# Squared-ReLU attention and a gated MLP on one core: the two key blocks of a pair share their keys in turn, queue order and buffers change

## The chip, the cores and the metric

One core of a Trainium2 chip runs the kernel. The metric is the device time of one launch in microseconds (us), from runs of the whole program. Five instruction streams run side by side: TensorE (PE, with its weight loads as PEld), VectorE (DVE), ScalarE (ACT), GpSimd (POOL) and SyncE (SP), which here issues nearly every DMA. Each works through its own instructions in order and waits for the others by semaphores.

## The reference

```python
scores = (1.0 / S) * np.matmul(z, z.transpose(0, 2, 1))   # z: 4 x 3008 x 64
attn = np.maximum(scores, 0.0) ** 2
x = (u * np.matmul(attn, v)).reshape(B * S, D)             # u, v: 4 x 3008 x 256
gate = 1.0 / (1.0 + np.exp(-(x @ w_gate)))                 # x: 12032 x 256, w_gate, w_val: 256 x 1536
out = (gate * (x @ w_val)) @ w_out                         # w_out: 1536 x 256
```

`u`, `v`, `z` are float32; the three weights are float64, and the kernel reads them as pairs of 32-bit words. The matrix of scores is symmetric, since both factors are z.

## The kernel before

Attention. Each of 4 batches has 6 chunks of queries (512, the last 448) and 12 pairs of key blocks (256 keys, the last pair 192). A step (b, c, i) is one pair i against one chunk c; there are 288, listed in `steps`, 12 for each chunk. TensorE makes the scores in two terms (lines 338, 339), ScalarE takes ReLU and square into a ring buffer `r` of four slots (346, 347), ScalarE or VectorE rounds to a high part `ah` (360, 362), VectorE forms the low part `al` (367), and TensorE multiplies both with the high and low parts of v (452, 454, 459). A chunk's sums stay in two banks of PSUM until `keep` copies them to DRAM (471, 472).

Symmetry is used. Where a pair's block e = i // 2 lies past the chunk c, the step's `r` is also wanted, transposed, by a later chunk. `turn` lets VectorE transpose 32 x 32 squares into one of six buffers `turned` (414), and `store` writes them by four DMAs to the DRAM tile `shared` (389). In the later chunk the step is mirrored: no scores are made, and `load_back` reads the block into its slot of `r` by two DMAs (429). `half` does the same for one quarter of the diagonal block (405, 423). In chunk (0, 0), called late, `r` is stored untransposed and turned after its read-back (434). In a row of the shared tile the 128 keys of one block lie side by side, so a store writes runs of 32 floats and a read-back reads runs of 128.

One turn g of the main loop emits: scores of step g + 2, the transpose and the stores of step g + 1, jobs listed in `before`, square and rounding of step g + 2, `keep` for a chunk that has ended, the read-back of step g + 4, jobs listed in `after`, and the products of step g. SP meets its DMAs in that order. Among the jobs are the loads of z and v for the next batch (into few raw buffers, 288) and 18 objects `Narrow`: each loads 512 KB of float64 weight words (178) in turn g, in turn g + 1 ScalarE takes their absolute value (183), and some turns later the float32 high and low parts are stored to DRAM (229, 230). They start at steps 24 to 52, 84 to 126 and 156 to 191, so batch 3 has none.

The gated MLP (called GLU in the code) follows in 12 groups of up to 1024 rows, six turns J each; its 12 pieces of weights `w_gv` and 6 of `w_o` are reloaded around the end of the attention (560, 562, 569). Rows of u and the sums are loaded a group ahead (497, 508). VectorE joins the products (610, 612) in ring order of four PSUM banks, and at a group's end `finish` transposes the outputs into `osb` (655), from where 16 DMAs write them (658); the second half (t = 1) uses the same two places as the first.

Of the kernel before, what the change touches and what calls it, by code (L numbers as in the profile page):

```python
# [26 lines left out]
def kernel(  # L27
# [10 lines left out]
    nc = tc.nc  # L38
# [15 lines left out]
    def chunk(c):  # L54
# [7 lines left out]
        "v": 68, "z": 28, "zq": 4, "r": 16, "ah": 12, "al": 8, "al2": 4,  # L62
# [49 lines left out]
    def shared(b, c, e):  # L112

        return e > c and ((b, c) != (0, 0) or e > 2)
# [5 lines left out]
    def order(b, c):  # L120
# [8 lines left out]
        own.sort(key=lambda i: (i // 2 != c, i))  # L129
# [29 lines left out]
    class Narrow:  # L159
# [64 lines left out]
        def parts(self):  # L224
# [4 lines left out]
            nc.sync.dma_start(dst[:, 0], f32(self.hi[:, 0:n]))  # L229
            nc.sync.dma_start(dst[:, 1], f32(self.lo[:, 0:n]))  # L230

        jobs = ("load", "abs", "shift", "sign", "low_words", "add", "sums", "parts")
# [45 lines left out]
    def v_place(b, i):  # L278
        n = (b * NPAIR + i) % 17
        hi, lo = part(v_a, 2 * n, CH, F32R), part(v_a, 34 + 2 * n, CH, F32R)  # L280
        return (ap.rearrange("p (j d) -> p j d", j=2) for ap in (hi, lo))

    def load_v(b, i):
# [3 lines left out]
        if i < NPAIR - 1:  # L287
            nc.sync.dma_start(t, v[b, k0 : k0 + 256, :].rearrange("(j p) d -> p j d", p=P))
# [25 lines left out]
    def r_of(s):  # L314
        return ring(r_a, 4, 4, s)

    def a_of(s):
        n = number[s] % 3
        al = part(al_a, 4 * n, 4 * KB, F32R) if n < 2 else part(al2_a, 0, 4 * KB, F32R)
        return ring(ah_a, 4, 3, s, F32R), al.rearrange("p (j q) -> p j q", j=2)  # L320

# [3 lines left out]
    def pe_scores(s):  # L325
# [10 lines left out]
        for j in range(2):  # L336
            o = (i % 2) * 256 + j * P
            nc.tensor.matmul(sc[:, j, 0 : n - q0], kh[:, o : o + P], q, start=True, stop=False)  # L338
            nc.tensor.matmul(sc[:, j, 0 : n - q0], kl[:, o : o + P], q, start=False, stop=True)  # L339
# [42 lines left out]
    shared_t, half_t = {}, {}  # L382

    def store(dst, t):

        rows = dst.rearrange("j (T p) q -> p (j T) q", p=32)
        for g in range(4):
            src = t[32 * g : 32 * g + 32].rearrange("p (T q) -> p T q", q=32)
            nc.sync.dma_start(rows[:, :, 32 * g : 32 * g + 32], src)  # L389
# [6 lines left out]
    def turn(s):  # L396
# [3 lines left out]
        e, r = i // 2, r_of(s)  # L400
        if halved(b, c) and i == 2 * c:
            half_t[b, c] = dram.tile([2, CH // 2, P], F32, name=f"half_{b}_{c}")
            t = turned(CH)
            for j in range(2):
                nc.vector.transpose(out=t[:, j * 256 : j * 256 + 256], in_=r[:, j, CH // 2 : CH])
            store(half_t[b, c], t)
        if shared(b, c, e):
            if (b, c, e) not in shared_t:
                shared_t[b, c, e] = dram.tile([4, CH, P], F32, name=f"shared_{b}_{c}_{e}")
# [529 lines left out]
```

## Time and profile before

| | us |
|---|---|
| median of 3 runs (lowest, highest) | 2238.66 (2236.91, 2243.06) |
| the profiled execution's own time | 2240.36 |
| its span, first to last instruction | 2238.6 |
| busy: TensorE, VectorE, ScalarE, GpSimd | 2018.6, 1362.7, 1106.3, 367.1 |

The span is read from one profiled execution; its time is 1.7 us above the median of the runs. TensorE's busy time is no measure of useful work alone, since a matmul takes twice as long at the lower of its two clock levels. TensorE's mean granted clock over the span is 0.956 of full speed. The attention fills about the first half of the span and the GLU the second.

### The profile page before, as it was taken

To read this page: it belongs to the slowest core of one execution; us is meant where nothing else is said; L and a number is where in the kernel's file an instruction comes from. 1 tells how busy PE (TensorE), PEld (TensorE's weight loads), DVE (VectorE), ACT (ScalarE), POOL (GpSimd) and SP (SyncE) were. 2 spreads that over 40 slices of the span, in tenths; PEclk is the share of its full clock that TensorE was granted. 3 is DMA by queue.
4 is the path that set the end of the run, shared out by engine and by line. 5 is a ranking of instruction groups with operands and counts; after the bars stand their busy time and mean duration, and the time that the engine had idled before them with its cause. 6 is when DMAs were issued, how large, how long until landed. Compare 5 with 4: busy or idle time off the path is not lost.

```text
span 2238.6 us, 25947 instructions
## 1 busy us (share of the span) xinstructions
PE 2018.6 (90%) x9078; PEld 1736.4 (78%) x9078; DVE 1362.7 (61%) x1719; ACT 1106.3 (49%) x1428; POOL 367.1 (16%) x293
## 2 busy tenths in 40 slices
PE   9987797886997779999699999999999999999998
PEld 7765586765876668887588888887888888888888
DVE  7565575665665556654466666566575666756654
ACT  8754375654666556775344334343343434434333
POOL 0000000000000000000023233232333332333323
PEclk9998999888998999999899999999999999999999
DMA  8786788877898877997841121111212112120110
GB/s 146 132 179 158 185 172 169 183 178 183 184 162 184 193 188 173 169 178 179 254 150 36 23 49 35 29 31 26 47 33 34 29 29 48 29 38 22 27 19 15
DMA packets 948611, 240.57 MB, mean 107 GB/s; under 512 B 780160, under 2 KB 922496, under 8 KB 948480
## 3 DMA queue, kind: packets, MB, share of 16 engines
q1 hardware_dynamic: 944224, 238.39, 49.4%
q8 instruction: 71, 1.16, 0.2%
q10 hardware_dynamic: 4256, 0.52, 0.1%
q14 instruction: 60, 0.49, 0.1%
HBM read 130.55 MB, written 102.24 MB: 104 GB/s over the span
## 4 chain that ended last, share of the span: by engine, by line
PE 61%; DMA 12%; SPq 10%; ACT 8%; DVE 5%; issue 4%; ACTq 0%; DVEq 0%
PE banks L587 10%; PE banks L589 10%; PE banks L588 10%; PE banks L648 5%; PE banks L649 5%; PE banks L647 5%; PE banks L452 4%; PE banks L459 4%; PE banks L454 4%; DMA r<-shared 4%; SPq L389 3%; ACT ah L362 3%; ACT r L347 2%; ACT r L346 2%; SPq L429 2%
## 5 line engine op out<-in xcount | busy, mean ns | idle before, releaser
L631 POOL TENSOR_TENSOR h<-spare,h 128x512 fp32r<-128x512 f32 (+1 forms) x288 | 366.7, 1273 | 1861.9 <-ACT h L626 1861.9
L452 PE MATMUL banks<-ah,v 128*128 128x512 f32 (+1 forms) x1152 | 457.9, 401 | 136.9 <-ACT ah L362 126.4
L367 DVE TENSOR_TENSOR al<-r,ah 128x1024 fp32r<-128x1024 f32 (+1 forms) x287 | 344.1, 1200 | 350.3 <-ACT ah L362 341.6
L454 PE MATMUL banks<-ah,v 128*128 128x512 f32 (+1 forms) x1104 | 434.5, 394 | 0.0
L459 PE MATMUL banks<-al,v 128*128 128x512 f32 (+1 forms) x1152 | 361.4, 397 | 25.5 <-DVE al L367 21.0
L452 PEld LDWEIGHTS banks<-ah,v 128*128 128x128 f32 x1152 | 230.8, 200 | 188.4 <-ACT ah L362 146.8
L622 DVE TENSOR_TENSOR spare<-banks,spare 128x512 f32<-128x512 f32 (+1 forms) x288 | 195.6, 679 | 287.5 <-PE banks L589 287.1
L362 ACT ACTIVATE ah<-r 128x1024 fp32r<-128x1024 f32 (+1 forms) x251 | 258.0, 1034 | 180.1 <-DMA r<-shared 139.0
L618 ACT ACTIVATE spare<-spare 128x512 f32<-128x512 f32 (+1 forms) x288 | 179.1, 622 | 326.5 <-DVE spare L612 320.3
L626 ACT ACTIVATE h<-spare 128x512 fp32r<-128x512 f32 (+1 forms) x288 | 178.6, 620 | 229.6 <-DVE spare L622 226.4
L459 PEld LDWEIGHTS banks<-al,v 128*128 128x128 f32 x1152 | 224.5, 199 | 77.0 <-DVE al L367 48.6
L454 PEld LDWEIGHTS banks<-ah,v 128*128 128x128 f32 x1104 | 222.4, 201 | 27.4
L346 ACT ACTIVATE r<-banks 128x1024 f32<-128x1024 f32 (+1 forms) x171 | 164.1, 959 | 41.5 <-PE banks L339 40.8
L347 ACT ACTIVATE r<-r 128x1024 f32<-128x1024 f32 (+1 forms) x171 | 172.0, 1006 | 5.4
L587 PE MATMUL banks<-z,v 128*128 128x512 f32 x414 | 157.2, 380 | 0.0
L589 PE MATMUL banks<-z,v 128*128 128x512 f32 x414 | 157.0, 379 | 0.0
L588 PE MATMUL banks<-z,v 128*128 128x512 f32 x378 | 143.3, 379 | 0.0
L338 PE MATMUL banks<-zq,z 128*128 128x512 f32 (+2 forms) x344 | 126.6, 371 | 10.4 <-DMA zq<-z 9.9
L612 DVE TENSOR_TENSOR spare<-banks,zt 128x512 f32<-128x512 f32 (+1 forms) x144 | 114.4, 794 | 31.8 <-PE banks L589 31.7
L612 DVE TENSOR_TENSOR spare<-banks,spare 128x512 f32<-128x512 f32 (+1 forms) x144 | 115.7, 804 | 27.3 <-PE banks L589 24.4
L587 PE MATMUL banks<-v 128*128 128x512 f32 (+1 forms) x342 | 126.9, 371 | 0.0
L588 PE MATMUL banks<-v 128*128 128x512 f32 (+1 forms) x342 | 126.7, 370 | 0.0
(120 smaller groups left out, 3235.6 us busy)
## 6 DMA issues: line engine op xcount, KB each, us to landing
r<-shared SPq DMA_DIRECT2D x220, 256.0 KB, 3.9
shared<-turned SPq DMA_DIRECT2D x292, 128.0 KB, 3.3
shared<-spare SPq DMA_DIRECT2D x148, 128.0 KB, 3.4
turned<-sums SPq DMA_DIRECT2D x22, 512.0 KB, 4.0
turned<-in_u_dram SPq DMA_DIRECT2D x176, 64.0 KB, 2.3
out_dram<-osb SPq DMA_DIRECT2D x176, 64.0 KB, 1.9
sums<-keep SPq DMA_DIRECT2D x20, 512.0 KB, 3.6
raw<-in_v_dram SPq DMA_DIRECT2D x33, 256.0 KB, 4.2
```

The source lines that it names most:

```text
L346: nc.scalar.activation(by_halves(r[:, :, q0:n]), products(sc[:, :, 0 : n - q0]), AF.Relu, scale=scale)
L347: nc.scalar.activation(r[:, :, q0:n], r[:, :, q0:n], AF.Square)
L362: nc.scalar.activation(ah[:, :, 0:n], r[:, :, 0:n], AF.Copy)
L367: nc.vector.tensor_tensor(al[:, :, 0:n], r[:, :, 0:n], f32(ah[:, :, 0:n]), op=ALU.subtract)
L452: nc.tensor.matmul(o, vh[:, j, ds], moving(ah[:, j, 0:n]), start=(k == 0 and j == 0), stop=False)
L454: nc.tensor.matmul(o, vl[:, j, ds], moving(ah[:, j, 0:n]), start=False, stop=False)
L459: nc.tensor.matmul(acc[:, d, 0:n], vh[:, j, ds], moving(al[:, j, 0:n]), start=False, stop=stop)
L587: nc.tensor.matmul(o, wt[:, 0, w], xh, start=(x == 0), stop=False)
L588: nc.tensor.matmul(o, wt[:, 0, w], xl, start=False, stop=False)
L589: nc.tensor.matmul(o, wt[:, 1, w], xh, start=False, stop=end)
L612: nc.vector.tensor_tensor(by_half(g_t[dst][:, 0:m]), product(bank(J, value, name)), product(other), op=ALU.add)
L631: nc.gpsimd.tensor_tensor(lo[:, 0:m], g_t[c][:, 0:m], f32(hi[:, 0:m]), op=ALU.subtract)
```

## The change

The keys of a pair are dealt to its two blocks in turn: key 2p goes to the first block and 2p + 1 to the second (the last pair stays as it was). The scores' weights are read with a step of two, v is loaded as two neighbouring rows to a partition, and the transposes write their squares interleaved. A shared tile is now 512 x 512 with whole rows, so a store writes runs of 64 floats (of 32 in the last pair), and one DMA reads a block back with two neighbouring rows to a partition. `r` has five slots for four, the v ring 16 places for 17, and block 5 of chunk (0, 0) is computed again and not shared. The late stores are issued by GpSimd.

In a turn, the read-back comes first and is that of step g + 5; then the store of a chunk's sums, one turn after its copy; then the stores of step g, transposed the turn before. The parts of narrowed weights are stored a turn later, at its end. Some of the last weights have other places and load at other times, and `finish` puts its second half into `t_p`. The diff, without its unchanged lines:

```diff
@@ -59,7 +59,7 @@
-        "v": 68, "z": 28, "zq": 4, "r": 16, "ah": 12, "al": 8, "al2": 4,
+        "v": 64, "z": 28, "zq": 4, "r": 20, "ah": 12, "al": 8, "al2": 4,
@@ -111,7 +111,7 @@
-        return e > c and ((b, c) != (0, 0) or e > 2)
+        return e > c and ((b, c) != (0, 0) or e in (3, 4))
@@ -126,7 +126,7 @@
-        own.sort(key=lambda i: (i // 2 != c, i))
+        own.sort(key=lambda i: (i // 2 > c, i // 2 < c and c < NCH - 1, i))
@@ -226,10 +226,15 @@
-            nc.sync.dma_start(dst[:, 0], f32(self.hi[:, 0:n]))
-            nc.sync.dma_start(dst[:, 1], f32(self.lo[:, 0:n]))
-        jobs = ("load", "abs", "shift", "sign", "low_words", "add", "sums", "parts")
+            self.done = [(dst[:, 0], f32(self.hi[:, 0:n])), (dst[:, 1], f32(self.lo[:, 0:n]))]
+        def store(self):
+            for dst, src in self.done:
+                nc.sync.dma_start(dst, src)
+        jobs = ("load", "abs", "shift", "sign", "low_words", "add", "sums", "parts", "store")
@@ -276,8 +281,8 @@
-        n = (b * NPAIR + i) % 17
-        hi, lo = part(v_a, 2 * n, CH, F32R), part(v_a, 34 + 2 * n, CH, F32R)
+        n = (b * NPAIR + i) % 16
+        hi, lo = part(v_a, 2 * n, CH, F32R), part(v_a, 32 + 2 * n, CH, F32R)
@@ -285,7 +290,7 @@
-            nc.sync.dma_start(t, v[b, k0 : k0 + 256, :].rearrange("(j p) d -> p j d", p=P))
+            nc.sync.dma_start(t, v[b, k0 : k0 + 256, :].rearrange("(p j) d -> p j d", j=2))
@@ -312,12 +317,17 @@
-        return ring(r_a, 4, 4, s)
+        return ring(r_a, 4, 5, s)
+    def keys_of(i, ap, j):
+        if i == NPAIR - 1:
+            return ap[:, j * P : j * P + P]
+        return ap.rearrange("p (n j) -> p j n", j=2)[:, j]
@@ -334,9 +344,10 @@
-            o = (i % 2) * 256 + j * P
-            nc.tensor.matmul(sc[:, j, 0 : n - q0], kh[:, o : o + P], q, start=True, stop=False)
-            nc.tensor.matmul(sc[:, j, 0 : n - q0], kl[:, o : o + P], q, start=False, stop=True)
+            o = (i % 2) * 256
+            h, l = (keys_of(i, ap[:, o : o + 256], j) for ap in (kh, kl))
+            nc.tensor.matmul(sc[:, j, 0 : n - q0], h, q, start=True, stop=False)
+            nc.tensor.matmul(sc[:, j, 0 : n - q0], l, q, start=False, stop=True)
@@ -379,14 +390,23 @@
-    shared_t, half_t = {}, {}
-    def store(dst, t):
-        rows = dst.rearrange("j (T p) q -> p (j T) q", p=32)
+    shared_t, half_t, turned_t = {}, {}, {}
+    def rows_of(d):
+        return d.rearrange("(T p) q -> p T q", p=32)
+    def store(dst, i, q0, t):
+        rows = rows_of(dst)
-            src = t[32 * g : 32 * g + 32].rearrange("p (T q) -> p T q", q=32)
-            nc.sync.dma_start(rows[:, :, 32 * g : 32 * g + 32], src)
+            src = t[32 * g : 32 * g + 32].rearrange("p (T q) -> p T q", q=64)
+            if i < NPAIR - 1:
+                nc.sync.dma_start(rows[:, :, q0 + 64 * g : q0 + 64 * g + 64], src)
+            else:
+                for j in range(2):
+                    q = q0 + P * j + 32 * g
+                    if q < chunk(NCH - 1):
+                        nc.sync.dma_start(rows[:, :, q : q + 32], src[:, :, 32 * j : 32 * j + 32])
@@ -397,41 +417,62 @@
-        e, r = i // 2, r_of(s)
+        e, r = i // 2, r_of(s).rearrange("p j (T a) -> p T j a", a=32)
-            half_t[b, c] = dram.tile([2, CH // 2, P], F32, name=f"half_{b}_{c}")
-            t = turned(CH)
-            for j in range(2):
-                nc.vector.transpose(out=t[:, j * 256 : j * 256 + 256], in_=r[:, j, CH // 2 : CH])
-            store(half_t[b, c], t)
-        if shared(b, c, e):
+            turned_t[s, "half"] = t = turned(CH)
+            nc.vector.transpose(out=t.rearrange("p (T b j) -> p T j b", j=2, b=32), in_=r[:, 8:16])
+        if shared(b, c, e) and not late(b, c):
+            turned_t[s] = t = turned(2 * CH)
+            lie = "p (T b j) -> p T j b" if i < NPAIR - 1 else "p (T j b) -> p T j b"
+            nc.vector.transpose(out=t.rearrange(lie, j=2, b=32), in_=r)
+    def store_turned(s):
+        b, c, i = s
+        if back(s):
+            return
+        e = i // 2
+        if (s, "half") in turned_t:
+            half_t[b, c] = dram.tile([CH // 2, CH // 2], F32, name=f"half_{b}_{c}")
+            store(half_t[b, c], 0, 0, turned_t.pop((s, "half")))
+        if not shared(b, c, e):
+            return
+        if late(b, c):
-                shared_t[b, c, e] = dram.tile([4, CH, P], F32, name=f"shared_{b}_{c}_{e}")
-            dst = shared_t[b, c, e][2 * (i % 2) : 2 * (i % 2) + 2]
-            t = r.rearrange("p j q -> p (j q)")
-            if not late(b, c):
-                src, t = t, turned(2 * CH)
-                nc.vector.transpose(out=t, in_=src)
-            store(dst, t)
+                shared_t[b, c, e] = dram.tile([CH // 2, 2 * CH], F32, name=f"shared_{b}_{c}_{e}")
+            rows, r = rows_of(shared_t[b, c, e]), r_of(s)
+            for g in range(4):
+                for j in range(2):
+                    o = 64 * (8 * (i % 2) + 2 * g + j)
+                    src = r[32 * g : 32 * g + 32, j].rearrange("p (T a) -> p T a", a=64)
+                    nc.gpsimd.dma_start(rows[:, :, o : o + 64], src)
+        else:
+            if (b, c, e) not in shared_t:
+                shared_t[b, c, e] = dram.tile([CH, CH], F32, name=f"shared_{b}_{c}_{e}")
+            store(shared_t[b, c, e], i, (i % 2) * 256, turned_t.pop(s))
+    def as_stored(i):
+        return part(keep_a, 4 * (i % 2), 2 * CH)
+        r = r_of(s)
-            r = r_of(s)
-            for j in range(2):
-                dst = r[:, j, 0 : CH // 2].rearrange("p (i q) -> p i q", q=P)
-                nc.sync.dma_start(dst, half_t[b, c][:, j * P : j * P + P, :].rearrange("i p q -> p i q"))
+            nc.sync.dma_start(r[:, :, 0 : CH // 2], half_t[b, c].rearrange("(p j) q -> p j q", j=2))
-            r = part(keep_a, 4 * (i % 2), 2 * CH).rearrange("p (j q) -> p j q", j=2) if late(b, i // 2) else r_of(s)
-            for j in range(2):
-                k0 = (i % 2) * 256 + j * P
-                dst = r[:, j].rearrange("p (i q) -> p i q", q=P)
-                nc.sync.dma_start(dst, shared_t[b, i // 2, c][:, k0 : k0 + P, :].rearrange("i p q -> p i q"))
+            n, d = chunk(c), shared_t[b, i // 2, c]
+            if late(b, i // 2):
+                nc.sync.dma_start(as_stored(i), d[P * (i % 2) : P * (i % 2) + P])
+            else:
+                rows = d[256 * (i % 2) : 256 * (i % 2) + 256].rearrange("(p j) q -> p j q", j=2)
+                nc.sync.dma_start(r[:, :, 0:n], rows[:, :, 0:n])
-            nc.vector.transpose(out=r_of(s).rearrange("p j q -> p (j q)"), in_=part(keep_a, 4 * (i % 2), 2 * CH))
+            src = as_stored(i).rearrange("p (B j a k) -> p k B j a", j=2, a=32, k=2)
+            dst = r_of(s).rearrange("p k (B b j) -> p k B j b", b=32, j=2)
+            for k in range(2):
+                nc.vector.transpose(out=dst[:, k], in_=src[:, k])
@@ -463,13 +504,15 @@
-    def keep(b, c):
+    def keep(b, c, store):
-        nc.scalar.activation(by_halves(t[:, :, 0:n]), products(acc_of(b, c)[:, :, 0:n]), AF.Copy)
-        nc.sync.dma_start(sums[:, :, t0 : t0 + n], t[:, :, 0:n])
+        if store:
+            nc.sync.dma_start(sums[:, :, t0 : t0 + n], t[:, :, 0:n])
+        else:
+            nc.scalar.activation(by_halves(t[:, :, 0:n]), products(acc_of(b, c)[:, :, 0:n]), AF.Copy)
@@ -547,9 +590,9 @@
-            a, o = v_a, (0, 28, 32, 36, 40, 44)[F]
+            a, o = v_a, (0, 4, 32, 36, 8, 12)[F]
-            a, o = (second("w", "wgv"), 7 * F) if F < 3 else (v_a, 4 + 7 * (F - 3))
+            a, o = (second("w", "wgv"), 7 * F) if F < 3 else (v_a, (16, 23, 40)[F - 3])
@@ -562,7 +605,7 @@
-        a, o = (v_a, 64) if F == 0 else (ah_a, 4 * (F - 1)) if F < 4 else (al_a, 4 * (F - 4))
+        a, o = (second("r", "x"), 16) if F == 0 else (ah_a, 4 * (F - 1)) if F < 4 else (al_a, 4 * (F - 4))
@@ -651,7 +694,7 @@
-        osb = part(second("al2", "osb"), 2 * h, CH)
+        osb = t_p[:, 2 + h] if t else part(second("al2", "osb"), 2 * h, CH)
@@ -678,13 +721,17 @@
+                if (b, p) == (1, 1):
+                    g = 5 * NPAIR + 3
+            for i in range(1, NPAIR):
+                line[i] = max(line[i], line[i - 1] + 1)
-                g = g0 + (2 * NPAIR + 4, 2 * NPAIR + 8, 3 * NPAIR + 2, 3 * NPAIR + 7, 4 * NPAIR + 6)[i] if i < 5 else line[i - 5]
+                g = g0 + (2 * NPAIR + 4, 2 * NPAIR + 8, 3 * NPAIR + 2, 3 * NPAIR + 7)[i] if i < 4 else line[i - 4]
@@ -696,7 +743,7 @@
-                at(after if x == 0 else before, g + x, getattr(job, name))
+                at(after if name in ("load", "store") else before, g + x, getattr(job, name))
@@ -708,7 +755,6 @@
-        at(after, g + 2, load_o, 0)
@@ -789,6 +835,11 @@
+            if g + 5 < len(steps):
+                load_back(steps[g + 5])
+            if k == 1 and g > 1:
+                keep(*steps[g - 2][:2], True)
+            store_turned(steps[g])
```

SP in batch 1, chunk 1, steps 90 to 93, before. `shared_1_5` is the tile of chunk 1 and block 5, `turned` and `spare` hold transposed squares, `w` the words of a narrowing job, and the row on `in_moe_w_gate_dram` is the load of one:

```order
L429 DMA r<-shared_0_1_1895 128x4x128 x2
L389 DMA shared_1_3_2258<-turned 32x32x32 x8
L389 DMA shared_1_4_2328<-spare 32x32x32 x8
L429 DMA r<-shared_0_1_1895 128x4x128 x2
L271 DMA zq<-z 64x512
L272 DMA zq<-z 64x512
L389 DMA shared_1_5_2384<-turned 32x32x32 x4
L229 DMA w_o<-w 128x512
L230 DMA w_o<-w 128x512
L423 DMA r<-half_1_2174 128x2x128 x2
L178 DMA w<-in_moe_w_gate_dram 128x2x512
L389 DMA shared_1_5_2384<-turned 32x32x32 x4
```

The same place after:

```order
L467 DMA r<-shared_0_1_1910 128x1024
L460 DMA r<-half_1_2189 128x2x256
L404 DMA shared_1_4_2343<-spare 32x16x64 x4
L276 DMA zq<-z 64x512
L277 DMA zq<-z 64x512
L404 DMA shared_1_4_2343<-spare 32x16x64 x4
L178 DMA w<-in_moe_w_gate_dram 128x2x512
L404 DMA shared_1_5_2395<-turned 32x16x64 x4
L233 DMA w_o<-w 128x512 x2
L467 DMA r<-shared_0_2_1961 128x1024
L409 DMA shared_1_5_2395<-turned 32x16x32 x6
```

The narrow load now stands ahead of all stores of `shared_1_5` and of the two `w_o` stores; the read-backs of `half` and of `shared_0_1` have moved up ahead of the stores of `shared_1_4`, and a read-back is one DMA where it was two.

SP at the start of the last chunk (3, 5), before: read-backs of `shared_*_5`, the first sums and rows of u, and weights (`w_gv`, `w_o`):

```order
L429 DMA r<-shared_0_5_5531 128x4x128 x4
L472 DMA sums<-keep 256x1x512
L429 DMA r<-shared_1_5_5802 128x4x128 x2
L497 DMA turned<-sums 128x2x512 x2
L508 DMA turned<-in_u_dram 32x16x32 x8
L560 DMA wgv<-w_gv 128x1792
L562 DMA v<-w_gv 128x2x512
L560 DMA wgv<-w_gv 128x1792
L429 DMA r<-shared_1_5_5802 128x4x128 x2
L429 DMA r<-shared_2_5_6048 128x4x128 x2
L508 DMA turned<-in_u_dram 32x16x32 x8
L569 DMA v<-w_o 128x1024
```

After:

```order
L467 DMA r<-shared_0_5_5483 128x2x448 x2
L467 DMA r<-shared_1_5_5750 128x2x448 x2
L540 DMA turned<-sums 128x2x512 x2
L551 DMA turned<-in_u_dram 32x16x32 x8
L603 DMA wgv<-w_gv 128x1792
L605 DMA v<-w_gv 128x2x512
L603 DMA wgv<-w_gv 128x1792
L467 DMA r<-shared_2_5_5998 128x2x448
L513 DMA sums<-keep 256x1x512
L467 DMA r<-shared_2_5_5998 128x2x448
L551 DMA turned<-in_u_dram 32x16x32 x8
L467 DMA r<-shared_3_5_6225 128x2x448 x2
```

Four mirrored steps are read back ahead of the sums where there were three, the load of `w_o` has left the place, and the chunk's own sums are stored later.

VectorE at the end of a group of the GLU, before, one row for the four output transposes:

```order
L655 STREAM_TRANSPOSE osb<-banks 128x512 x4
```

After:

```order
L698 STREAM_TRANSPOSE osb<-banks 128x512 x2
L698 STREAM_TRANSPOSE turned<-banks 128x512 x2
```

Two of the four now go to `turned`, whose upper half is `t_p`.

## Rows read from the trace of the kernel before

**Rows 1.** Stages: us; busy of PE, PEld, DVE, ACT, POOL (count); clock, DMA share, GB/s.
```profile
94.10:263.10 169.00, 125.80 (x500) 102.46 (x499) 93.93 (x114) 87.08 (x97) 0.00 (x0) 0.87 0.72 166
263.10:303.80 40.70, 34.76 (x160) 29.90 (x159) 21.87 (x26) 20.82 (x26) 0.00 (x0) 0.96 0.67 186
303.80:344.40 40.60, 40.60 (x192) 35.64 (x191) 31.03 (x32) 32.07 (x33) 0.00 (x0) 1.00 0.92 161
344.40:555.90 211.50, 164.53 (x674) 134.89 (x673) 122.26 (x148) 116.27 (x130) 0.00 (x0) 0.88 0.81 180
555.90:592.80 36.90, 33.29 (x160) 30.58 (x159) 19.50 (x24) 20.07 (x26) 0.00 (x0) 0.95 0.71 193
633.40:838.70 205.30, 163.41 (x674) 132.91 (x673) 119.58 (x142) 115.54 (x128) 0.00 (x0) 0.91 0.82 183
838.70:874.80 36.10, 32.97 (x160) 30.90 (x159) 18.50 (x22) 19.85 (x25) 0.00 (x0) 0.95 0.66 182
915.30:1071.60 156.30, 149.23 (x678) 124.83 (x677) 84.64 (x78) 103.63 (x107) 0.00 (x0) 1.00 0.87 175
1071.60:1120.50 48.90, 29.36 (x116) 25.36 (x115) 21.32 (x22) 14.60 (x17) 0.00 (x0) 0.77 0.93 271
1120.50:2238.60 1118.10, 1072.09 (x4996) 942.75 (x4995) 702.75 (x976) 434.65 (x694) 366.69 (x288) 0.99 0.18 37
```

**Rows 2.** Waits of ScalarE for DMA, whole span: total us, times, longest.
```profile
ACT ah L362 <- DMA r<-shared: 139.0, 42, 15.3
ACT v L297 <- DMA raw<-in_v_dram: 60.0, 20, 7.4
ACT w L183 <- DMA w<-in_moe_w_val_dram: 52.8, 6, 12.1
ACT w L183 <- DMA w<-in_moe_w_out_dram: 43.2, 6, 11.5
ACT w L183 <- DMA w<-in_moe_w_gate_dram: 40.5, 6, 11.2
```

**Rows 3.** Timeline around one narrowing job: start, us, engine, line, operation [idle before].
```profile
347.95 2.24 SPq L389 DMA_DIRECT2D shared<-turned  x4
371.09 6.51 SPq L389 DMA_DIRECT2D shared<-spare  x8
380.24 3.15 SPq L389 DMA_DIRECT2D shared<-turned  x4
385.62 0.53 SPq L178 DMA_DIRECT2D w<-in_moe_w_gate_dram  x1
...
373.49 1.24 DVE L414 STREAM_TRANSPOSE spare<-r 128x1024 f32<-128x1024 f32 x1
...
378.10 1.06 ACT L362 ACTIVATE ah<-r 128x1024 fp32r<-128x1024 f32 x1
390.39 0.66 ACT L183 ACTIVATE w<-w 128x512 f32<-128x512 f32 x1 [11.23 <-DMA w<-in_moe_w_gate_dram]
...
392.05 0.80 PE L452 MATMUL banks<-ah,v 128*128 128x512 f32 x1 [7.63 <-ACT ah L362]
```

**Rows 4.** DMA packets from 895 to 899 us, stores only.
```profile
DMA packets 5456, 0.69 MB, mean 172 GB/s; under 512 B 5456, under 2 KB 5456, under 8 KB 5456
```

**Rows 5.** DMA packets from 1048 to 1052 us, nearly all read-backs.
```profile
DMA packets 2392, 1.19 MB, mean 297 GB/s; under 512 B 75, under 2 KB 2392, under 8 KB 2392
```

**Rows 6.** DMA from 793 to 797 us, nearly all of 2 KB: packets, MB, share.
```profile
q1 hardware_dynamic: 560, 1.05, 76.1%
```

**Rows 7.** Waits of TensorE at the GLU's group ends, whole span.
```profile
PE banks L587 <- DVE zt L610: 38.9, 11, 4.2
```

**Rows 8.** Groups by line: busy us, mean ns | idle before, releaser.
```profile
L338 PEld LDWEIGHTS banks<-zq,z 128*128 128x128 f32 x344 | 65.9, 192 | 22.3 <-DMA zq<-z 12.1 <-ACT zq L744 1.4 <-issue 0.3
L414 DVE STREAM_TRANSPOSE turned<-r 128x1024 f32<-128x1024 f32 x73 | 90.4, 1238 | 0.0
L655 DVE STREAM_TRANSPOSE osb<-banks 128x512 f32<-128x512 f32 (+1 forms) x48 | 32.3, 693 | 55.3 <-DMA out_dram<-osb 53.0 <-PE banks L649 2.3
```

More of the change, by code (lines that the diff above doesn't have):

```diff
@@ L803 @@
             if k == 0 and g:
-                keep(*steps[g - 1][:2])
-            if g + 4 < len(steps):
-                load_back(steps[g + 4])
+                keep(*steps[g - 1][:2], False)
             run(after, g)
@@ L839 @@
                 at(extra, (J + 7, 0), finish, G - 1, 1, h)
-        for i in (6, 9, 11, 8):
+        at(extra, (0, 0), load_o, 0)
+        for i in (9, 11, 6, 10):
             at(extra, (0, 1), load_w, i)
-        at(extra, (0, 2), load_w, 10)
-        at(extra, (0, 2), keep, *steps[-1][:2])
+        at(extra, (0, 2), load_w, 8)
+        at(extra, (0, 2), keep, *steps[-1][:2], False)
+        at(extra, (0, 2), keep, *steps[-1][:2], True)
         for F in range(1, NF):
```

## The prediction, made before the changed kernel was run

> **What bounds the kernel now.** I read the page's slices first, to see where TensorE's granted clock falls; that is in the first half. Then I cut the span into stages [rows 1]: the attention, up to about 1120 us, has the stretches with a lower clock, and the GLU behind it runs at 0.99. The boundaries are the starts of chunks on TensorE. A first chunk (303.8 to 344.4) has TensorE busy for the whole 40.60 us at full clock: 0.2157 us for a matmul of 512 columns (40.6 us for 186 of these and 4 of half the width, by the code). Batch 3's chunks 1 to 4 take 156.3 us for 678 matmuls; the same work takes 211.5 us in batch 1 and 205.3 us in batch 2, with the clock at 0.88 and 0.91, and three such chunks of batch 0 take 169.0 us for 500. What batch 3 lacks are the 18 narrowing jobs (float64 weights read, split, written back) and the loads for a next batch. DMA is no sufficient bound: in batch 3's first chunks its share is no lower (0.87) than where TensorE starves (0.72 to 0.82).
>
> The waits say who starves it [rows 2]: ScalarE sat 136.5 us (52.8 + 43.2 + 40.5) before the first operation of these 18 jobs, 139.0 us for 42 read-backs and 60.0 us for 20 loads of v. ScalarE works in order, so a wait there holds back the rounding on which TensorE's next product depends. One such job shows the cause [rows 3]: ScalarE is done with its step at 379.16 and waits 11.23 us; TensorE then waits 7.63 us. The load was issued only at 385.62, because SP, in order, had first to issue eight stores (6.51 us), a read-back, two copies of z, four more stores (3.15 us) and three other transfers. Stores come at 0.8 us each there, not at the 0.56 of four issued beside little other traffic (2.24 us at 347.95), and 0.8 us is about what the DMA engines need for one: 5456 packets of 128 bytes in 4 us over 16 engines is 11.7 ns each, and a store has 1024 [rows 4].
>
> **The change part by part.** *Queue order.* In a turn of the loop SP now issues the read-back for five steps ahead before anything else, then the stores of the step transposed one turn earlier. So SP no longer waits for a transpose of the same turn, and the narrow load moves ahead of four stores, two stores of the previous job and a read-back. For the job of rows 3: the step whose stores now precede the load has its transpose done at 374.73 (373.49 + 1.24). Four stores at 0.56 us put the load at about 377.0; it lands 4.7 us later (385.62 to 390.39 today, with the wait's end), near 381.7. ScalarE would wait 2.5 us instead of 11.2, and TensorE ran dry only at 384.42 (392.05 - 7.63): nothing of its wait is left.
>
> I price this by batch 3 as a measure. Its pace is 156.3 / 678 = 0.2305 us. Batch 0 lost 169.0 - 500 x 0.2305 = 53.7 us against it, batch 1 211.5 - 674 x 0.2305 = 56.1 us, batch 2 49.9 us: 159.7 us together. The load is still issued only about a turn and a half before its use, and not every job has the slack of this one. I leave 1.7 us for each of the 18 jobs, 30 us: **130 us saved**. Bounds: 80 us (half the excess stays) and 159.7.
>
> *Read-backs.* Batch 3's pace itself lies above TensorE's own: 662 x 0.2157 + 16 x 0.108 = 144.5 us against 156.3, an excess of 11.8 us, which is 44 us over 3.7 such groups (2526 matmuls against 678). Its waits are read-backs. They now get one step more of lead and stand ahead of the stores. I take two thirds: **29 us**, bounds 10 and 44. The fifth ring slot pays for it; the v ring shrinks from 17 to 16 places, which puts one v load a step later. The chunks 5 (40.7, 36.9, 36.1 us) hold 160 matmuls each, 30.2 us at 0.189 us for 448 columns: 23 us of excess. There a v load still waits for its own buffer and SP with it, so I take half, **11.5 us** (0 to 23). Two steps of (0, 5) are now computed, not mirrored: 8 matmuls, **1.5 us lost**; their rounding lies beside products.
>
> *DMA runs.* No row shows a 256-byte packet. Below it is 11.7 ns for 128 bytes [rows 4], above it 26.8 ns for 512 (2392 packets in 4 us [rows 5]); between them, a third of the way up, 17 ns. A step's four stores then take 2048 x 17 / 16 = 2.2 us instead of 4096 x 11.7 / 16 = 3.0. A read-back in 4 KB runs takes at most two 2 KB packets each (560 packets at a share of 0.761 of 4 us are 87 ns [rows 6]): 128 x 174 / 16 = 1.4 us instead of 1024 x 26.8 / 16 = 1.7. Over some 115 stored and as many read steps that frees about 130 us of DMA time. I add nothing for it: it is what lets SP's stores come at 0.56 us, and in rows 1 TensorE ran all but full beside shares of 0.87 to 0.92.
>
> At this place the Trainium skill speaks against the change: "DMA: Bandwidth & Descriptors", section Specifications, says transfers need 512 bytes for line rate and that below it the engine reads, modifies and writes. Where the rows show 11.7 ns at 128 bytes against 26.8 at 512, no such surcharge is seen on the small ones; the trace so far disagrees. By that rule a 256-byte store could cost as much as two of 128, which is rival three.
>
> *Last chunk.* 48.9 us for 116 matmuls (22 us at 0.19), DMA share 0.93. Its volume hardly changes: read-backs cost some 0.3 us less for 10 steps, and the 16 loads of u and the weights stay. Read-backs past the first four still queue behind weights. I take **10 us** (0 to 20).
>
> *GLU.* The second pair of output transposes wrote where the first pair's stores were still being read: VectorE waited 53.0 us for output stores [rows 8], and TensorE 38.9 us in 11 places for VectorE's joins [rows 7]. Now they write into t_p, free by then (T3 and T4 were rounded a step before; the next turn_u is a step later, about 14 us). Four transposes of 0.693 us [rows 8] then run in a row, 2.8 us, beside products already queued. I take the 38.9 us plus 6 of the 11 us by which a clock of 0.99 lengthens 1118 us: **45 us** (30 to 50).
>
> *Priced at nothing.* Interleaved keys: weight loads of the scores read every second element, 192 ns today [rows 8] behind matmuls of 216; the moving operand already steps between two halves at full pace. Bounds: 0, and at twice the duration (384 - 216) x 696 = 117 us. Interleaved transposes: 1238 ns contiguous for 1024 columns, while L655 reads every second element at 693 for 512, 12% above half of that; at worst 0.15 us on 110 steps of VectorE, 16 us, in its idle time (it is busy 84.64 of 156.3 us in batch 3, 122.26 of 211.5 in batch 1). Late stores on GpSimd: 32 issues where it was idle. No row shows its issue time; at SP's 0.56 us they take 18 us beside the first chunks, at 2 us some would hold a ring slot and cost up to 35.
>
> **Sum.** 130 + 29 + 11.5 - 1.5 + 10 + 45 = 224 us. The profiled execution took 2240.4 us for a span of 2238.6; 2240.4 - 224 = 2016. The median of the runs is 1.7 us below it: **2015 us**.
>
> **The rivals.** *The narrow loads stay late*: abs still follows its load by one turn, and if SP's own issuing keeps it from running ahead, half the excess stays. Savings 80 + 15 + 5 - 1.5 + 0 + 45 = 144, so 2095 us. For it: four stores at 0.56 us, a read-back and the copies fill some 3 us of a computed step's 3.5 (16 matmuls). Against: rows 3 place the load 8 us earlier.
>
> *Everything goes*: 159.7 + 44 + 23 - 1.5 + 15 + 50 = 290, so 1949 us. For it: first chunks run at TensorE's pace with DMA at 0.92. Against: 18 loads of 512 KB with so short a lead.
>
> *The runs don't get cheaper*, at the price of two 128-byte packets: a step's stores stay at 3 us of DMA and 0.8 us an issue; each narrow load comes 1 us later, 18 us: 2033 us.
>
> *Slower: interleaved weights.* The 696 score matmuls become bound by their weight loads, at L (duration) - 216 ns each. Against savings of 224 us it decides from 216 + 224000 / 696 = 538 ns, 2.8 times today's; at 600 ns the time is 2015 + 267 = 2282 us. For it: no row shows a strided weight load. Against: strided reads of VectorE and of the moving side cost 12% or nothing.
>
> **Chances.** Forecast 0.62, narrow loads late 0.16, everything 0.11, runs not cheaper 0.04, no change (gains and an unpriced wait cancel) 0.02, slower 0.05. That gives faster 0.93, within 0.3% (what measurement can't tell from no change) 0.02, slower 0.05. The range 1960 to 2100 holds the forecast with its bounds, most of the first rival and the third.
>
> **What would show it.** ScalarE's waits before the abs operation fall from 136.5 us to under 50; those for r<-shared from 139 to under 40; batches 1 and 2 take about 165 us for chunks 1 to 4; TensorE's waits for L610's successor vanish; stores show 17 ns a packet; score matmuls keep 0.216 us. Wrong: ScalarE still waiting 5 us or more per narrow load, SP blocked for long at its first read-back of a turn, or gaps at the score matmuls.

## The result and the profile after

The changed kernel takes 2026.49 us (median of 4 runs, 2024.75 to 2028.90) where the kernel before takes 2240.86 (4 runs, 2236.91 to 2245.31): a ratio of 0.9044, 95% interval 0.9022 to 0.9065. Forecast were 2015 us, 1960 to 2100. The profiled execution of the changed kernel took 2024.75 us with a span of 2022.6, at a mean granted clock of 0.987 (before 0.956).

The stages of the changed kernel, cut at the same places of the program as [rows 1] (us; busy of PE, PEld, DVE, ACT, POOL with counts; granted clock, DMA share, GB/s):

```profile
94.20:233.80 139.60, 116.29 (x499) 95.37 (x499) 95.05 (x114) 86.42 (x97) 0.00 (x0) 0.94 0.73 196
233.80:266.30 32.50, 32.28 (x168) 31.28 (x167) 20.27 (x25) 24.55 (x31) 0.00 (x0) 1.00 0.67 192
306.90:474.40 167.50, 153.73 (x673) 130.80 (x672) 124.48 (x144) 115.75 (x128) 0.00 (x0) 0.95 0.86 225
474.40:505.50 31.10, 30.90 (x160) 29.60 (x159) 21.71 (x27) 21.44 (x27) 0.00 (x0) 1.00 0.68 209
546.10:707.80 161.70, 150.86 (x673) 127.54 (x672) 122.20 (x138) 115.12 (x127) 0.00 (x0) 0.98 0.89 229
707.80:738.20 30.40, 30.40 (x160) 29.86 (x159) 20.41 (x26) 20.92 (x26) 0.00 (x0) 1.00 0.66 197
778.80:922.90 144.10, 144.10 (x677) 127.17 (x676) 87.57 (x73) 104.53 (x107) 0.00 (x0) 1.00 0.76 189
922.90:959.10 36.20, 23.53 (x113) 21.84 (x111) 19.02 (x20) 11.86 (x13) 0.00 (x0) 0.86 0.93 293
959.10:2022.60 1063.50, 1056.71 (x5000) 933.60 (x4998) 705.61 (x978) 437.22 (x696) 366.89 (x288) 1.00 0.19 41
```

Chunks 1 to 4 of batch 3 now stand at TensorE's own pace: 144.10 us, all busy at full clock, where [rows 1] has 156.3. Batch 1 needs 167.5 us for them (211.5 before), batch 2 161.7 (205.3), batch 0 139.6 (169.0): 129.2 us less in all four. The three chunks 5 lost 8.2, 5.8 and 5.7 us, together 19.7. The first GLU matmul starts at 960.42 us, 37.5 us after the last chunk's start (50.1 before, 1071.6 to 1121.68), so 12.6 us less; from it to the end are 1062.2 us, where there were 1116.9, so 54.7 us less. That makes the 216 us by which the span fell.

ScalarE's waits for DMA in the changed kernel (total us, times, longest), the answer to [rows 2]:

```profile
ACT v L302 <- DMA raw<-in_v_dram: 35.5, 25, 3.6
ACT w L183 <- DMA w<-in_moe_w_gate_dram: 27.5, 6, 8.4
ACT ah L373 <- DMA r<-shared: 19.9, 4, 10.0
ACT w L183 <- DMA w<-in_moe_w_val_dram: 18.1, 6, 6.3
ACT w L183 <- DMA w<-in_moe_w_out_dram: 16.7, 6, 4.3
```

The read-backs are nearly gone from the list (139.0 us before; 19.9 now, in four waits of the last chunk), the narrow loads (the three rows of L183) fell from 136.5 to 62.3 us, v from 60.0 to 35.5. TensorE's waits for ScalarE's rounding (`PE banks <- ACT ah`) fell from 126.4 us to 44.5, and no wait for the GLU's joins is left.

The job of [rows 3], step 91, in the changed kernel (start, us, engine, line, operation, idle before):

```profile
329.23 2.35 SPq L404 DMA_DIRECT2D shared<-spare  x4
331.68 0.72 SPq L276 DMA_DIRECT2D zq<-z  x1
332.44 1.04 SPq L277 DMA_DIRECT2D zq<-z  x1
333.57 2.28 SPq L404 DMA_DIRECT2D shared<-spare  x4
335.90 0.52 SPq L178 DMA_DIRECT2D w<-in_moe_w_gate_dram  x1
...
330.91 1.61 DVE L427 STREAM_TRANSPOSE spare<-r 128x1024 f32<-128x1024 f32 x1
...
333.89 1.06 ACT L373 ACTIVATE ah<-r 128x1024 fp32r<-128x1024 f32 x1
340.57 0.66 ACT L183 ACTIVATE w<-w 128x512 f32<-128x512 f32 x1 [5.62 <-DMA w<-in_moe_w_gate_dram]
...
342.23 0.48 PE L493 MATMUL banks<-ah,v 128*128 128x512 f32 x1 [2.03 <-ACT ah L373]
```

The transpose ahead of the load (L427) ends at 332.52, but SP is then still at two copies of z (L276, L277); it issues the stores from 333.57 and the load at 335.90. ScalarE is done at 334.95 and waits 5.62 us, not 11.23; TensorE waits 2.03 us, not 7.63.

### The profile page after: what moved, and what is told of

It is laid out like the page before. It is cut to its first block, busy times and chain, and to the rows that moved or that the text cites. A ratio compares the mean times of both kernels' runs of the same rounds, so it can differ in the third digit from the quotient of the medians.

```text
span 2022.6 us, 25614 instructions
## 1 busy us (share of the span) xinstructions
PE 1951.4 (96%) x9086; PEld 1710.3 (85%) x9086; DVE 1381.6 (68%) x1702; ACT 1115.9 (55%) x1432; POOL 386.9 (19%) x325
## 3 DMA queue, kind: packets, MB, share of 16 engines
q0 software_dynamic: 1024, 2.10, 0.5%
## 4 chain that ended last, share of the span: by engine, by line
PE 74%; DMA 7%; SPq 6%; ACT 5%; DVE 5%; issue 3%; DVEq 0%; ACTq 0%
PE banks L631 11%; PE banks L632 11%; PE banks L630 11%; PE banks L500 6%; PE banks L493 6%; PE banks L690 6%; PE banks L692 6%; PE banks L691 6%; PE banks L495 6%; ACT ah L373 2%; PE banks L350 2%; PE banks L349 2%; DVE al L378 2%; SPq L404 2%; DMA w<-in_moe_w_out_dram 2%
## 5 line engine op out<-in xcount | busy, mean ns | idle before, releaser
L493 PE MATMUL banks<-ah,v 128*128 128x512 f32 (+1 forms) x1152 | 437.8, 383 | 45.5 <-ACT ah L373 44.5
L495 PE MATMUL banks<-ah,v 128*128 128x512 f32 (+1 forms) x1104 | 419.7, 380 | 0.0
L500 PE MATMUL banks<-al,v 128*128 128x512 f32 (+1 forms) x1152 | 347.8, 384 | 16.1 <-DVE al L378 13.7
L493 PEld LDWEIGHTS banks<-ah,v 128*128 128x128 f32 x1152 | 222.1, 193 | 81.8 <-ACT ah L373 53.0
L373 ACT ACTIVATE ah<-r 128x1024 fp32r<-128x1024 f32 (+1 forms) x251 | 255.4, 1032 | 51.3 <-DMA r<-shared 19.9
L500 PEld LDWEIGHTS banks<-al,v 128*128 128x128 f32 x1152 | 218.4, 193 | 56.7 <-DVE al L378 30.7
L495 PEld LDWEIGHTS banks<-ah,v 128*128 128x128 f32 x1104 | 212.5, 192 | 25.3
L357 ACT ACTIVATE r<-banks 128x1024 f32<-128x1024 f32 (+2 forms) x173 | 167.0, 965 | 94.5 <-PE banks L350 91.8
L358 ACT ACTIVATE r<-r 128x1024 f32<-128x1024 f32 (+2 forms) x173 | 174.4, 1008 | 5.5
L655 DVE TENSOR_TENSOR spare<-banks,spare 128x512 f32<-128x512 f32 (+1 forms) x144 | 117.9, 819 | 27.2 <-PE banks L632 24.2
L655 DVE TENSOR_TENSOR spare<-banks,zt 128x512 f32<-128x512 f32 (+1 forms) x144 | 116.4, 808 | 28.8 <-PE banks L632 28.7
L349 PE MATMUL banks<-zq,z 128*128 128x512 f32 (+2 forms) x348 | 126.7, 367 | 1.5 <-DVE zq L792 1.5
L350 PE MATMUL banks<-zq,z 128*128 128x512 f32 (+2 forms) x348 | 126.8, 367 | 0.0
L630 PE MATMUL banks<-v 128*128 128x512 f32 (+1 forms) x342 | 126.6, 370 | 0.0
```

Source lines behind the costliest of these rows:

```text
L373: nc.scalar.activation(ah[:, :, 0:n], r[:, :, 0:n], AF.Copy)
L493: nc.tensor.matmul(o, vh[:, j, ds], moving(ah[:, j, 0:n]), start=(k == 0 and j == 0), stop=False)
L495: nc.tensor.matmul(o, vl[:, j, ds], moving(ah[:, j, 0:n]), start=False, stop=False)
L500: nc.tensor.matmul(acc[:, d, 0:n], vh[:, j, ds], moving(al[:, j, 0:n]), start=False, stop=stop)
L630: nc.tensor.matmul(o, wt[:, 0, w], xh, start=(x == 0), stop=False)
L655: nc.vector.tensor_tensor(by_half(g_t[dst][:, 0:m]), product(bank(J, value, name)), product(other), op=ALU.add)
```

## The experiments

All runs in this section are of whole kernels, made in three groups with the kernel before beside each: its median was 2254.68 us beside e1 to e4, 2250.43 beside e5 to e7 and 2250.98 beside e8, against 2240.86 beside the changed kernel. Times of one group compare directly; across groups I go by the ratio to the kernel before (0.01 is about 22.5 us), or leave some 10 us open.

| kernel | median us | ratio to before (95%) |
|---|---|---|
| changed kernel | 2026.49 | 0.9044 (0.9022 to 0.9065) |
| e1_glu_place | 2193.19 | 0.9741 (0.9706 to 0.9775) |
| e2_order_short_runs | 2062.69 | 0.9165 (0.9127 to 0.9203) |
| e3_runs_old_order | 2168.06 | 0.9638 (0.9600 to 0.9676) |
| e4_narrow_early | 1995.75 | 0.8866 (0.8834 to 0.8898) |
| e5_weights_early | 1989.07 | 0.8837 (0.8813 to 0.8861) |
| e6_stores_later | 2026.13 | 0.9003 (0.8975 to 0.9031) |
| e7_loads_first | 2073.61 | 0.9212 (0.9187 to 0.9237) |
| e8_read_back_last | 1978.90 | 0.8792 (0.8778 to 0.8807) |

**The GLU's places alone** (e1_glu_place), in the kernel before:

```diff
-        osb = part(second("al2", "osb"), 2 * h, CH)
+        osb = t_p[:, 2 + h] if t else part(second("al2", "osb"), 2 * h, CH)
```

Expected:

> The kernel before with one edit: the second half of a group's outputs is transposed into t_p and not into the places that the first half's stores still read. Theory (a wait of its own in the GLU, independent of the attention): the whole 54.7 us by which the GLU got shorter comes from here, 2241 - 54 = 2187 us, TensorE's 38.9 us of waits for the joins gone, attention as long as before. Rival (the GLU gained by other weight places and loads, or by a clock that the busier attention left behind): under 30 us, 2211 us or more.

2193.19 us, 61 us under the kernel before beside it (51 to 66 by the interval). TensorE's waits of 10 us and more in this kernel (total us, times, longest):

```profile
PE banks L452 <- ACT ah L362: 135.1, 41, 9.5
PE banks L459 <- DVE al L367: 20.6, 14, 7.4
PE banks L338 <- DMA zq<-z: 12.0, 8, 2.9
```

The row of [rows 7], the GLU matmul waiting for a join, is gone, and the attention's waits stand as before. From the first GLU matmul (1130.09 us) to the end are 1061.1 us, as in the changed kernel (1062.2), where the kernel before has 1116.9. So the GLU's gain is this edit's, and it adds to the attention's.

**Order without long runs, and long runs without the order.** e2_order_short_runs is the changed kernel with the old layout, its core:

```diff
-            nc.sync.dma_start(t, v[b, k0 : k0 + 256, :].rearrange("(p j) d -> p j d", j=2))
+            nc.sync.dma_start(t, v[b, k0 : k0 + 256, :].rearrange("(j p) d -> p j d", p=P))
...
+        rows = dst.rearrange("j (T p) q -> p (j T) q", p=32)
         for g in range(4):
...
+            src = t[32 * g : 32 * g + 32].rearrange("p (T q) -> p T q", q=32)
+            (eng or nc.sync).dma_start(rows[:, :, 32 * g : 32 * g + 32], src)
```

> The changed kernel with the old layout: keys of a pair in order, stores in runs of 128 bytes, read-backs in runs of 512 bytes by two DMAs; the new order of the queue, the fifth slot, the places and all else stay. Theory Q (the order of the queue brings the attention's gain, the longer runs little): about 2055 us, ScalarE's waits for r<-shared under 60 us. Theory R (the DMA time of short runs is what held the queue up): most of the attention's 161 us is lost again, 2130 us or more, with stores issued at 0.8 us each.

e3_runs_old_order keeps the layout and undoes the order in a turn (that the weights' parts are stored where they are made again is not shown):

```diff
-            if g + 5 < len(steps):
-                load_back(steps[g + 5])
-            if k == 1 and g > 1:
-                keep(*steps[g - 2][:2], True)
-            store_turned(steps[g])
             turn(steps[g + 1])
+            store_turned(steps[g + 1])
...
                 keep(*steps[g - 1][:2], False)
+                keep(*steps[g - 1][:2], True)
+            if g + 4 < len(steps):
+                load_back(steps[g + 4])
```

> The changed kernel with the old order in a turn: transpose and stores of step g+1 first, then the copy and store of a chunk's sums, then the read-back of step g+4, and the weights' parts stored where they are made; layout, slots and places stay. Theory Q: most of the attention's gain is lost, about 2130 us, ScalarE waiting again over 100 us for its narrow loads. Theory R: the long runs carry the gain, 2060 us or less.

2062.69 us and 2168.06 us. The changed kernel without its order loses about 140 us (142 by the medians, 134 by the ratios), without its long runs about 30 (36 and 27). e3 came out 38 us above theory Q's forecast: beside e1, which has the GLU's edit alone and took 2193.19 us in the same group, the long runs, the fifth slot and the other places together bring only 25 us as long as the old order stands. ScalarE's waits, first of e2, then of e3:

```profile
ACT v L302 <- DMA raw<-in_v_dram: 56.3, 28, 4.7
ACT w L183 <- DMA w<-in_moe_w_gate_dram: 29.7, 6, 9.4
ACT w L183 <- DMA w<-in_moe_w_val_dram: 22.9, 6, 7.3
ACT w L183 <- DMA w<-in_moe_w_out_dram: 22.3, 6, 6.0
ACT ah L371 <- DMA r<-shared: 19.3, 3, 12.8
```

```profile
ACT ah L370 <- DMA r<-shared: 132.1, 36, 14.2
ACT w L183 <- DMA w<-in_moe_w_val_dram: 50.6, 6, 10.0
ACT w L183 <- DMA w<-in_moe_w_out_dram: 41.8, 6, 10.5
ACT w L183 <- DMA w<-in_moe_w_gate_dram: 39.0, 6, 10.0
```

With the old order the waits are about those of the kernel before (139.0 and 136.5), 132.1 us for read-backs and 131.4 for narrow loads, although the runs are long. With short runs in the new order the read-backs still come in time (19.3 us); narrow loads wait 74.9 us (62.3 in the changed kernel) and v 56.3 (35.5). Theory Q holds: the order carries the attention. In the new order the runs bring some 30 us; ScalarE's waits for v and narrow loads are 33.4 us longer without them. This is a net figure: e2 also has the old transposes, which are shorter (1238 ns), and two DMAs for a read-back.

**Which half of the order?** e6_stores_later returns the read-back, of step g + 4, to its old place; e7_loads_first returns the stores to their transpose's own turn:

```diff
-            if g + 5 < len(steps):
-                load_back(steps[g + 5])
...
+            if g + 4 < len(steps):
+                load_back(steps[g + 4])
             run(after, g)
```

> The changed kernel, but the read-back is that of step g+4 again and stands where it stood, behind the stores; the stores stay one turn later. Theory S (what counts is that no transfer stands behind a transpose of its own turn): nearly all of the 141 us stays won, 2045 us or less. Rival L (the read-backs' own place and lead carry it): 2100 us or more, with ScalarE waiting over 80 us for r<-shared.

```diff
-            store_turned(steps[g])
             turn(steps[g + 1])
+            store_turned(steps[g + 1])
```

> The changed kernel, but the stores are those of step g+1 again, right behind their transpose; the read-back of step g+5 stays first in the turn. Theory S: the narrow and v loads are late again, 2110 us or more, although the waits for r<-shared stay under 40 us. Rival L: 2060 us or less.

2026.13 and 2073.61 us. With the stores a turn later the kernel has all that the order wins; with the read-backs first it has some two thirds (about 95 us of 135 to 140, across two groups), a time between the two forecasts, so theory S gave that half too little. The two halves overlap: either brings most of the gain alone. Both kernels also keep what e3 undid besides, the late stores of a chunk's sums and of the weights' parts; no run tests those alone, so part of either share may be theirs. ScalarE's waits for read-backs and v in e6, and TensorE's for ScalarE's rounding in it; then ScalarE's in e7:

```profile
ACT ah L373 <- DMA r<-shared: 62.9, 28, 14.6
ACT v L302 <- DMA raw<-in_v_dram: 22.2, 20, 2.5
PE banks L493 <- ACT ah L373: 49.4, 17, 9.4
```

```profile
ACT v L302 <- DMA raw<-in_v_dram: 61.4, 26, 7.4
ACT w L183 <- DMA w<-in_moe_w_val_dram: 34.9, 6, 7.1
ACT w L183 <- DMA w<-in_moe_w_out_dram: 32.0, 6, 8.2
ACT w L183 <- DMA w<-in_moe_w_gate_dram: 26.0, 6, 7.3
ACT ah L373 <- DMA r<-shared: 19.3, 4, 10.1
```

In e6 ScalarE waits 62.9 us for read-backs, 43 us more than in the changed kernel, for narrow loads 62.5 us as there and for v less (22.2 us), and the time is the same within what two groups can tell. The 28 waits are 2.2 us each on average, one of them 14.6, and TensorE's waits for ScalarE's rounding grew only from 44.5 to 49.4 us: most of the 43 us lie where TensorE still had products queued. A wait of ScalarE is no loss by itself; the slack behind it decides. In e7 the read-backs are in time, but narrow loads (92.9 us) and v (61.4 us) again stand behind stores that wait for VectorE: SP waits 77.7 us at its stores (L404) for transposes into `turned` there, 9.6 in the changed kernel.

**The rest at the narrow loads** (e4_narrow_early), in the changed kernel:

```diff
-                at(after if name in ("load", "store") else before, g + x, getattr(job, name))
+                at(after if name in ("load", "store") else before, g + x - (x == 0), getattr(job, name))
```

> The changed kernel with the 18 loads of narrowing jobs issued one turn earlier, all else the same. Theory (what is left over TensorE's pace in batches 0 to 2, some 74 us, stands mostly at these loads, 62.3 us of ScalarE's waits): the waits fall under 20 us and the time to about 1985 us. Rival (the load only hides other late transfers: v, z, the stores in front): ScalarE then waits elsewhere, 2015 us or more.

1995.75 us, a ratio of 0.8866 against 0.9044 for the changed kernel. The waits for narrow loads fell to about 16 us (8.6, 4.7 and 2.4); ScalarE now waits mainly for v:

```profile
ACT v L302 <- DMA raw<-in_v_dram: 47.1, 28, 4.8
ACT ah L373 <- DMA r<-shared: 17.7, 3, 11.0
```

The theory's mechanism held. It had forecast 41 us less than the changed kernel; measured are 31 by the medians and 40 by the ratios, across groups.

**Weights out of the last chunk** (e5_weights_early), on top of e4:

```diff
-        for i in (0, 1, 2):
-            at(after, g, load_w, i)
+        for x, i in enumerate((0, 1, 2, 3, 4, 5, 7)):
+            at(after, g - 23 + 3 * x, load_w, i)
...
-        for i in (3, 4, 5, 7):
-            at(after, g + 4, load_w, i)
```

> The kernel with the early narrow loads (e4_narrow_early), and seven of the GLU's weight loads (0 to 5 and 7) moved from the last chunk to steps 253, 256, ... 271 of batch 3. Theory (the last chunk's gap, where ScalarE waits 17.7 us for r<-shared, is DMA time of weights and rows of u queued ahead of read-backs): 1985 us, these waits under 8 us. Rival (the gap stems from the rows of u alone, whose stores of 128-byte runs hold SP for 19 us): 1993 us or more, the wait as it was.

1989.07 us, between the two forecasts, and the intervals of e4 and e5 overlap; the waits for r<-shared fell from 17.7 us to 12.6, not under 8. Not decided by the time. The traces say a little more: from the copy of the sums before the last chunk (L515) to the first GLU matmul are 30.8 us (894.3 to 925.05), in e4 37.4 (895.9 to 933.36), so most of the 8 us between the two profiled executions lies in this chunk, and the weights were part of its gap. That the rows of u are the rest is not shown.

**Read-backs last** (e8_read_back_last), on top of e5: the two lines of the read-back of step g + 5 moved behind `run(after, g)`.

> e5_weights_early with the read-back of step g+5 moved from the first to the last place of a turn, behind the stores and the loads of v, z and narrowing jobs. Theory (with stores a turn late, the place of the read-backs is worth nothing, since they have five steps of lead; the loads of v, with the shortest lead, gain by standing ahead of them): ScalarE's waits for v fall from 51.2 us to under 35, time 1975 to 1987 us. Rival (read-backs behind a v load that waits for its buffer come too late): waits for r<-shared over 60 us, 2000 us or more.

1978.90 us, the best of all, 0.8792 (0.8778 to 0.8807) of the kernel before. Its waits of ScalarE:

```profile
ACT v L302 <- DMA raw<-in_v_dram: 40.5, 22, 3.9
ACT ah L373 <- DMA r<-shared: 30.5, 23, 4.6
```

The time is as the theory said; the wait for v fell to 40.5 us, not under 35, and that for read-backs rose to 30.5 without costing time. So read-backs that are five steps ahead gain nothing from the first place of a turn. The 10 us that the last place won over e5 are about what I leave open across groups, though the two intervals just miss each other; what won them is not shown.

## Why the prediction was right, and where its sizes were off

*What bounds the kernel.* Right: ScalarE held up by late loads, behind SP's order. e3 against e6 shows it: long runs with the old order leave the waits about as they were (132.1 us for read-backs, 131.4 for narrow loads), and with the stores out of their transpose's turn both halve (62.9 and 62.5).

*Queue order, 130 us, and read-backs, 29 us.* Together they brought 129.2 us in chunks 1 to 4, 30 less than forecast. The read-back term was too small: batch 3 lost all of its excess (156.3 to 144.1 us), not two thirds. So the narrow term was mis-sized. Taking the read-backs' 44 us as all won, it brought some 85 us instead of 130. That is the size that the first rival gave this term (80), and not the forecast's: against batch 3's new pace (144.1 / 677 = 0.213 us a matmul) batches 0 to 2 still lose 33 + 24 + 18 = 76 us, half of the 159.7. ScalarE's waits at the narrow loads are 62.3 us, not under 50, or 3.5 us a job.

The step that failed is the one on the job of [rows 3], that four stores at 0.56 us right behind the transpose put the load 2.2 us before ScalarE is done. It came 0.95 us after. Some 2.0 us of the difference are VectorE's: the transpose ended 2.43 us before ScalarE's step and not 4.43, since it began later against that step and took 1.61 us, not 1.24. Some 1.05 us are SP's: it was still issuing the copies of z (0.72 and 1.04 us), which the forecast weighed in its first rival alone. From issue to use the load took 4.7 us, as forecast. This is one job of 18; the others were not taken apart. e4 shows that about half of the 76 us lay in this lead: one turn more wins 31 us by the medians, 40 by the ratios. Where the rest lies stays open.

*A sign of being wrong that came.* The prediction named SP blocked for long at its first read-back of a turn. SP's three largest waits at these read-backs (L467) come to 109.3 us (total us, times, longest); in the kernel before the largest is 23.8 (L429, 10 times):

```profile
SPq L467 <- DVE turned L423: 56.0, 12, 9.2
SPq L467 <- DVE al L378: 27.2, 18, 4.0
SPq L467 <- DVE turned L427: 26.1, 10, 5.6
```

A read-back five steps ahead writes the slot of `r` that the present step holds (five slots), so SP waits until VectorE, by these rows the last to read it, is done. The waits at the stores have in part moved to the first DMA of the turn. That costs little here: e6, whose read-backs come behind the stores, takes the same time, and e8 took 10 us off e5.

*DMA runs.* Between the bounds, nearer to the interpolation of 17 ns than to two short packets (23.4): with nothing but stores in the queue (748 to 752 us of the changed kernel)

```profile
DMA packets 3342, 0.83 MB, mean 207 GB/s; under 512 B 3342, under 2 KB 3342, under 8 KB 3342
```

makes 4 us x 16 / 3342 = 19.2 ns for a packet of 256 bytes, against 11.7 for 128 in [rows 4] and 26.8 for 512 in [rows 5]. The forecast added nothing of its own for the runs, which it held part of the queue's term; its third rival priced runs that get no cheaper at 18 us, and e2 measures some 30 without the long runs. The rule of "DMA: Bandwidth & Descriptors" of the Trainium skill (Specifications), line rate from 512 bytes on and a read-modify-write below, agrees in that 256 bytes move at 207 GB/s and 512 at 297 [rows 5], though the first are stores and the second read-backs; a step between them that would show the read-modify-write is not seen.

*Chunks 5 and the last chunk.* 11.5 - 1.5 us forecast, 19.7 measured; 10 forecast, 12.6 measured. The longest read-back wait that is left in the last chunk (10.0 us, to 940.14) stands behind sums, rows of u and weights, which SP issued from 921.78 to 931.56 us, ahead of this read-back.

*GLU.* 45 us forecast, 54.7 measured. From its first matmul to the end TensorE's idle time fell from 46.0 to 6.8 us, the 38.9 us of waits, and its busy time from 1070.9 to 1055.4 as the granted clock rose from 0.99 to 1.00. So 15.5 us came back with the clock, where the forecast took 6 of 11. e1 shows both (busy 1054.9, clock 1.00), so neither needs the changed attention.

*Priced at nothing.* These rows answer [rows 8] (busy us, mean ns of one, idle before; the last two rows give ns min/median/max instead, and the very last is of the kernel before):

```profile
L349 PEld LDWEIGHTS banks<-zq,z 128*128 128x128 f32 x348 | 68.1, 196 | 9.3 <-ACT zq L790 2.0
L427 DVE STREAM_TRANSPOSE turned<-r 128x1024 f32<-128x1024 f32 x73 | 107.9, 1478 | 0.0
L447 POOL DMA_DIRECT2D shared<-r x32 | 19.6, 621 | 29.8 <-ACT r L358 29.8
L427 DVE STREAM_TRANSPOSE turned<-r x73: 1211/1533/1623, 62.3 to 907.8; 128x1024 f32<-128x1024 f32 x73
L260 DVE STREAM_TRANSPOSE zt<-raw x18: 669/711/726, 162.2 to 848.2; 128x512 f32<-128x512 f32 x18
```

Weight loads with a step of two take 196 ns (192 before), so the slower rival's 538 ns are far off. The mean of 1478 ns mixes two kinds of transposes: the last pair's, whose output is contiguous, take 1.24 us as before (19 of 110), the interleaved ones 1.41 to 1.62 us, 1.54 on average (91). That is 24% above 1238, twice the 12% of the forecast's bound. The bound was misread: it set L655's 512 columns with a step of two against half of 1024 contiguous ones, but 512 contiguous columns take 711 ns too (L260). So no cost of reading from PSUM with a step of two was seen, and no row showed what writing with one costs. VectorE had room for it in batch 3, which runs at TensorE's pace with 87.57 of 144.1 us busy; in the job above the longer transpose was 0.4 us of the lead. GpSimd issues its stores in 621 ns, near SP's 0.56 us.

*The sum.* 224 us forecast, 216 measured: about -45 on the narrow term, +15 on the read-backs, +10, +3 and +10 on the others. That the savings came within 8 us and the time within 12 (2026.49 us against 2015) is luck in part: the largest term brought a third less than forecast, and four smaller ones that brought more made up for most of it.

## What to carry to other kernels

Where one queue issues the loads and the stores, look first for a store that waits for work of its own turn: everything behind it inherits that wait, and moving the stores a turn back won more here (135 to 140 us, with those of the sums and weights) than doubling the length of their runs (about 30). Give each load the lead that its consumer's slack needs, and count what the issuing engine still has in hand before it, not only when its data is ready. A load that is put first waits too, if its buffer is still being read. A wait of an engine off the bound is a loss only past the work that is queued for the bound.

## What the runs showed of the hardware that was not expected

A transpose of 128 x 1024 floats on VectorE whose output goes to every second element takes 1.54 us on average (1.41 to 1.62, 91 of them); with a contiguous output and the input read in the same order it takes 1.24 us (19), as in the kernel before (1238 ns). Reading every second element of PSUM showed no cost: 128 x 512 took 707 ns so (L655, median) and 711 ns contiguous from SBUF (L260). In packets of 256 bytes the 16 DMA engines moved 207 GB/s, in packets of 128 bytes 172 GB/s [rows 4]: doubling the run gave only a fifth more, 19.2 ns instead of 11.7 for a packet.
